# Reading a corner sum from PSUM, and moving two chunks' loads, in a fused attention and MLP kernel

## The chip, the cores and the metric

The kernel runs on one core of one Trainium2 chip. The metric is the device time of one execution in microseconds (us); the time given for a kernel is the median over several executions. One execution was also taken with the hardware profiler, and its trace is what this document reads. The engines are called as in the trace: PE is TensorE's matmul and PEld its weight load, DVE is VectorE, ACT is ScalarE, POOL is GpSimd, SP is the engine that only issues DMAs here.

## The reference

Linear attention with decay over 4 batches, 8 heads, 768 positions and head size 64, followed by a two-layer MLP (512 to 2048 to 512) with ELU between the layers:

```python
for b in range(nb):                                   # blocks of positions
    intra = einsum('bhic,bhjc->bhij', qb, kb) * Dmask # causal, lam ** (i - j)
    intra = einsum('bhij,bhjd->bhid', intra, vb)
    inter = einsum('bhid,bhde->bhie', qb * lam_pow, kv_state)
    out[:, :, sl] = intra + inter
    kv_state = lam_block * kv_state + einsum('bhsd,bhse->bhde', kb * rev_pow, vb)
x = out.transpose(0, 2, 1, 3).reshape(3072, 512)      # tokens x (heads * 64)
h = x @ w_in
g = where(h > 0, h, exp(min(h, 0)) - 1)
return g @ w_out                                      # float32, 3072 x 512
```

## The kernel before

The kernel works on 24 chunks of 128 tokens. Chunk g holds batch g % 4 and positions g // 4 * 128 onward. Chunks 0 to 3 go through the MLP alone, the others in pairs, named by the first of the two ("group 12" is chunks 12 and 13). Everything is float16 in SBUF with float32 sums in PSUM.

**Attention of a chunk.** `emit_load` loads q, k and v with DMAs issued by POOL (line 107), two chunks per DMA from chunk 4 on. From chunk 8 on, `pool_work` (token `W`) issues the DMA transposes of q and k on SP (line 270), scales k on POOL (kd, line 176) and scales the old state (stt, line 390 on POOL, line 383 on ACT). Scores are PE line 304 (token `S`), the masking of scores is DVE line 320 (pp), the outputs are PE lines 340 and 346 (token `P`), the state update is PE line 417 with DVE line 440 (token `U`). The scores of both chunks of a pair stand next to each other on PE.

**The MLP.** `mm1` computes 512 columns of the first layer into one of two PSUM buffers psH (PE line 660), then ACT takes the exponential (line 666, e) and the relu in place (line 667), and DVE forms ELU from the two (line 626, called g or gg), which sets psH free. For chunks 0 to 7 the second layer is plain (`mm2`, line 685). For the pairs from 8 on, `mm2_seven` (line 549) multiplies by Strassen's seven products: the 2 x 2 blocks are the two chunks by the two halves of the 512 output columns. The sums of gg that the products need (fp, fd, fe) are formed by `sums` on DVE (line 500) or POOL (line 497), the sums of the weights (wf) by `w_sums` (line 517).

**The corner sums.** The products come in the order m3, m4, m5, m2, m1, m7, m6, with first-layer matmuls between them, into halves of two PSUM banks. m5 adds up on m3 in the same half bank, m2 on m4, m6 on m1. ACT copies m3, m4 and m1 to SBUF (line 556, `keep`), and copies the two corners that m5 and m2 complete into the output tiles osb (line 566, `corner`). POOL adds t = m3 + m4, and subtracts the corners from t (s1 and s2, line 562, written into the buffers of m3 and m4). DVE adds w1 = s1 + m1 (line 562), and closes the other two corners with w1 - m7 and s2 + m6 (line 579), each of which reads one operand from PSUM.

**Order.** The order on every engine is written by hand. `OPEN` is the list of tokens for the first part of the program: `W8` is `pool_work(8)`, `L12` loads chunks 12 and 13, `S8:9` does scores, `1:g:j` and `2:g:j` are parts of `mm1` and `mm2`. After it the same tokens are placed at fixed distances from the first-layer steps (`AT`). Small DVE operations wait in the lists `late`, `slow` and `later`, which `flush` works off at each following step; `late.insert(0, ...)` puts one first. `COMB` is POOL.

Of the kernel before, what the change touches and what calls it, by code (L numbers as in the profile page):

```python
# [7 lines left out]
FP32 = mybir.dt.float32  # L8
# [3 lines left out]
ALU = mybir.AluOpType  # L12
# [3 lines left out]
def kernel(  # L16
# [11 lines left out]
    nc = tc.nc  # L28
    out_dram = out

    B, H, S, D = q.shape
# [28 lines left out]
    )  # L60
    LAGU = 13
    LATE = 4
# [2 lines left out]
    COMB = nc.gpsimd  # L65
# [15 lines left out]
    msb = ctx.enter_context(tc.tile_pool(name="msb", bufs=1))  # L81
# [29 lines left out]
    for w in RAW.split():  # L111
        x = {"q": q, "k": k}[w[0]]
        g0 = int(w[1:])
        raw[w] = asb.tile([128, H, 64], FP32, name=f"raw_{w}", tag=f"raw_{w}")
        (nc.sync if w[0] == "q" else nc.scalar).dma_start(
            out=raw[w][:], in_=x[g0, :, 0:L].rearrange("h p d -> p h d")
# [84 lines left out]
    def zero_st1(b):  # L201
# [21 lines left out]
        out=ident16[:], in0=row[:], scalar1=pos[:, 0:1], scalar2=None, op0=ALU.is_equal  # L223
    )
    nc.vector.tensor_scalar(
        out=causT[:], in0=row[:], scalar1=pos[:, 0:1], scalar2=None, op0=ALU.is_ge
# [82 lines left out]
    late, X_done, Y_done, E_done = [], set(), set(), set()  # L309
# [209 lines left out]
    L_, R_ = slice(0, 256), slice(256, 512)  # L519
    later, sides = [], [0, 1]  # L520

    def mm2_seven(g0, i):
        flush()
        while slow and i in (2, 4, 5):
            slow.pop(0)()
        if i == 0:
            seven[g0] = {}
            sides.reverse()
        z = seven[g0]
        if i < 2:  # L530
            while later:
                later.pop(0)[1]()
            z[f"bank{i}"] = ps.tile(
                [128, DM], FP32, tag=f"psM{sides[i]}", name=f"psM{g0 + i}", bufs=1
            )
        m = (3, 4, 5, 2, 1, 7, 6)[i]
        half = L_ if i < 4 else R_
        out = z["bank1" if m in (4, 2, 7) else "bank0"][:, half]
        for s in range(NFT // 2):
            t = g2[(g0, s // 2)]  # L540
            p, d, e = forms[(g0, s // 2)]
            u = s % 2
            lhs = {3: t[:, u, 0, 0, :], 4: t[:, u, 1, 1, :], 1: e[:, u, :], 7: d[:, u, 1, :],
                   6: d[:, u, 0, :], 5: p[:, u, 0, :], 2: p[:, u, 1, :]}[m]
            if m in (5, 2):
                rhs = wo16[s][:, 1, R_] if m == 5 else wo16[s][:, 0, L_]
            else:
                rhs = wf[s][:, (3, 4, 1, 6, 7).index(m), :]
            nc.tensor.matmul(  # L549
                out, lhsT=lhs, rhs=rhs, start=(s == 0 and m in (3, 4, 1, 7)),  # L550
                stop=(s == NFT // 2 - 1), skip_group_check=True,
            )

        def keep(n):
            z[n] = msb.tile([128, 256], FP32, tag=n, bufs=1, name=f"{n}_{g0}")
            nc.scalar.copy(out=z[n][:], in_=out)  # L556

        def comb(n, in0, in1, op, into=None, eng=None):
            z[n] = z[into] if into else msb.tile(
                [128, 256], FP32, tag=n, bufs=1, name=f"{n}_{g0}"  # L560
            )
            (eng or COMB).tensor_tensor(out=z[n][:], in0=in0, in1=in1, op=op)  # L562

        def corner(c, half):
            z[c] = msb.tile([128, DM], FP32, tag="osb512", bufs=4, name=f"osb{g0 + c}")
            nc.scalar.copy(out=z[c][:, half], in_=out)  # L566
            if last:
                store(c, half)

        last = g0 == NG - 2  # L570

        def store(c, cols):
            cb, b = divmod(g0 + c, B)
            t0 = b * S + cb * L
            stores.append((out_dram[t0 : t0 + 128, cols], z[c][:, cols]))

        def last_of(c, half, x, op):
            def one():
                nc.vector.tensor_tensor(out=z[c][:, half], in0=z[x][:], in1=out, op=op)  # L579
                store(c, half if last else slice(0, DM))  # L580
                C_done.add(g0 + c)

            later.append([DELAY, one])


        if m == 3:
            keep("m3")
        elif m == 4:
            keep("m4")
            comb("t", z["m3"][:], z["m4"][:], ALU.add)  # L590
        elif m == 5:
            corner(0, R_)
            comb("s1", z["t"][:], z[0][:, R_], ALU.subtract, "m3")
        elif m == 2:
            corner(1, L_)
            comb("s2", z["t"][:], z[1][:, L_], ALU.subtract, "m4")
        elif m == 1:
            keep("m1")
            late.insert(
                0, lambda: comb("w1", z["s1"][:], z["m1"][:], ALU.add, "m1", nc.vector)  # L600
            )
        elif m == 7:
            last_of(0, L_, "w1", ALU.subtract)
        else:
            last_of(1, R_, "s2", ALU.add)
# [6 lines left out]
    def flush():  # L612
        while pending:
            g0, j, e, r = pending.pop(0)
            n = GSIZE[g0]
            if g0 in SEVEN:
                if j % 2 == 0:
                    g2[(g0, j // 2)] = msb.tile(
                        [128, 2, 2, 2, 128], FP16, tag="g2", bufs=8, name=f"gg{g0}_{j}"
                    )  # L620
                g = g2[(g0, j // 2)][:, j % 2]
            else:
                g = msb.tile(
                    [128, FB // n, n, 128], FP16, tag="g", bufs=24, name=f"g{g0}_{j}"
                )[:]
            nc.vector.scalar_tensor_tensor(  # L626
                out=g.rearrange("p f c t -> p (f c t)"), in0=e[:], scalar=-1.0, in1=r[:],
                op0=ALU.add, op1=ALU.min,
            )
            for f in range(FB // n):  # L630
                for c in range(n):
                    gts[(g0 + c, j * (FB // n) + f)] = g[:, f, c, :]
            if g0 in SEVEN and j % 2 == 1:
                slow.extend(sums(g0, j // 2))
        if late:
            late.pop(0)()
        if slow and len(late) < 2:
            slow.pop(0)()
        for x in later:
            x[0] -= 1  # L640
        while later and later[0][0] <= 0:
            later.pop(0)[1]()
# [82 lines left out]
    def run(t):  # L725
# [13 lines left out]
        if w == "S":  # L739
            for g in a:  # L740
                att_S(g)
            for g in a:
                late.extend(att_E(g))
            late.pop(0)()
            late.pop(0)()
        elif w == "P":
            burst(t)
        elif w == "U":
            late.extend(att_U(*a))
            while late:  # L750
                late.pop(0)()
        else:
            {"T": att_T_pe, "1": mm1, "2": mm2, "Z": zero_st, "z": zero_st1,
             "q": lambda g, e: cast_raw(g, "q", e), "k": lambda g, e: cast_raw(g, "k", e),
             "7": mm2_seven, "F": w_sums, "G": lambda i: w_sums(i, nc.gpsimd), "c": lambda i: (emit_qs, emit_mask, emit_ks)[i](), "W": pool_work,
             "M": next_M}[w](*a)
# [7 lines left out]
    m1 = [(g, j) for g, n in GSIZE.items() for j in range(NJ * n)]  # L764
# [14 lines left out]
    for g in range(0, NG, 2):  # L779
        u = place[(GFIRST[g], 0)] - (8 if GSIZE[GFIRST[g]] == 4 and g == GFIRST[g] else 0)  # L780
# [14 lines left out]
    m1 = [x for x in m1 if "1:%d:%d" % x not in done]  # L795
# [4 lines left out]
    for x, (g, j) in enumerate(m1):  # L800
        u = first + x
# [3 lines left out]
        n = 2 if back > LAGU and m2[0][0][0] == "2" else 1  # L805
# [44 lines left out]
```

## Time and profile before

| | before |
|---|---|
| median of 8 runs | 218.33 us (215.33 to 220.48) |
| the profiled execution | 216.19 us |
| its span in the trace | 214.4 us |
| PE busy | 196.8 us, 92% of the span |
| DVE busy | 163.2 us, 76% |
| POOL busy | 160.9 us, 75% |
| ACT busy | 140.6 us, 66% |

The span runs from the first to the last instruction of the program; the execution's time has 1.8 us around it. In a row of groups or of the timeline the columns are: start and duration in us, engine, line of the code, operation, output and inputs by the program's names with their shapes and the number of instructions; in brackets stands how long the engine was idle before it and what ended that. In the list of waits each row has the waiting engine and line, the releaser, and the total, the number and the longest of the waits in us. In the chain of waits each row is a start, a duration and what held the chain there. An engine's name with a q is its queue: there the time that an issue takes is shown, and a DMA's row in the chain reaches from its issue to its landing.

### The profile page before, as it was taken

Reading aid. Unit: us, or ns where it says so; the run is one execution under the profiler, and the core shown is the slowest. Engines: PE = TensorE matmul, PEld = TensorE weight load, DVE = VectorE, ACT = ScalarE, POOL = GpSimd, SP = SyncE. Lnnn points to the kernel's source line nnn. Section 1 sums busy time; section 2 is a strip of 40 time slices with the busy share of each in tenths; the row PEclk is TensorE's granted clock in tenths of the full one; section 3 lists DMA queues with packets and bytes.
Section 4 is the critical chain, followed back from the end, with each engine's and each line's share of the span. In section 5 each row is a group of like instructions: output and inputs, shape, how many; then the busy total and the mean of one; then the engine's idle time right before and its main releaser. Section 6 shows DMA issues by size and latency. Waiting matters only on the chain.

```text
span 214.4 us, 5659 instructions
## 1 busy us (share of the span) xinstructions
PE 196.8 (92%) x2224; PEld 157.4 (73%) x2224; DVE 163.2 (76%) x294; ACT 140.6 (66%) x285; POOL 160.9 (75%) x187
## 2 busy tenths in 40 slices
PE   0689999999999997999999999979999999999983
PEld 0467767858586764667887887968888888888862
DVE  3864571689947785998979889898999989886622
ACT  4537665874875772867876867866567667677730
POOL 7999799999999999685999999995370301205961
PEclk9999999999999999999999999999999999999999
DMA  8999999999992399189719979979999911011032
GB/s 87 131 166 191 196 195 186 160 185 186 143 151 73 22 175 171 29 94 112 140 16 150 127 95 151 159 52 140 148 78 152 130 52 49 3 49 49 3 113 82
DMA packets 102122, 24.61 MB, mean 115 GB/s; under 512 B 92624, under 2 KB 99280, under 8 KB 102096
## 3 DMA queue, kind: packets, MB, share of 16 engines
q0 software_dynamic: 79760, 13.50, 82.9%
q1 hardware_dynamic: 22336, 10.76, 26.9%
q8 instruction: 17, 0.28, 0.6%
q14 instruction: 9, 0.07, 0.1%
HBM read 27.27 MB, written 6.29 MB: 157 GB/s over the span
## 4 chain that ended last, share of the span: by engine, by line
PE 70%; DMA 8%; DVE 8%; ACT 6%; POOL 5%; issue 2%; ACTq 0%; DVEq 0%; POOLq 0%; SPq 0%
PE psH L660 31%; PE psM L549 20%; PE psM L685 11%; DMA wo<-in_moe_w_out_dram 4%; DMA kT<-kn 4%; DVE gg L626 3%; PE psS L304 3%; ACT e L666 3%; ACT psH L667 3%; PE psO L340 2%; PE psO L346 2%; POOL wi L149 1%; POOL vn L107 1%; POOL kn L107 1%; DVE m L562 1%
## 5 line engine op out<-in xcount | busy, mean ns | idle before, releaser
L660 PE MATMUL psH<-xt,wi 128*128 128x256 f16 (+1 forms) x896 | 100.7, 260 | 3.6 <-DVE gg L626 2.3
L660 PEld LDWEIGHTS <-wi 128*128 128x128 f16 x896 | 78.6, 99 | 18.9 <-issue 4.9
L666 ACT ACTIVATE e<-psH 128x512 f32<-128x512 f32 x96 | 57.3, 597 | 47.9 <-PE psH L660 46.6
L667 ACT ACTIVATE psH<-psH 128x512 f32<-128x512 f32 x96 | 57.0, 593 | 0.0
L626 DVE SCALAR_TENSOR_TENSOR gg<-e,psH 128x512 f16<-128x512 f32 x64 | 43.6, 681 | 13.7 <-ACT psH L667 13.4
L320 DVE TENSOR_TENSOR pp<-psS,mask 128x512 f16<-128x512 f32 x48 | 31.3, 682 | 5.4 <-PE psS L304 5.4
L626 DVE SCALAR_TENSOR_TENSOR g<-e,psH 128x512 f16<-128x512 f32 x32 | 21.9, 684 | 17.3 <-ACT psH L667 17.1
L685 PE MATMUL psM<-wo,g 128*128 128x512 f16 x128 | 32.1, 379 | 0.1
L497 POOL TENSOR_TENSOR fd<-gg 128x512 f16<-128x512 f16 x20 | 24.6, 1232 | 2.8 <-DVE gg L626 2.7
L176 POOL TENSOR_TENSOR kd<-kn,ks 128x512 f16<-128x512 f16 x20 | 21.4, 1073 | 1.7 <-DMA kn<-in_k_dram 1.6
L497 POOL TENSOR_TENSOR fe<-gg 128x256 f16<-128x256 f16 x16 | 12.2, 764 | 13.0 <-DVE gg L626 12.9
L517 POOL TENSOR_TENSOR wf<-wo 128x256 f16<-128x256 f16 (+1 forms) x28 | 21.1, 792 | 0.1
L562 POOL TENSOR_TENSOR t<-m,m 128x256 f32<-128x256 f32 x8 | 5.8, 726 | 19.6 <-ACT m L556 19.6
L685 PEld LDWEIGHTS <-g 128*128 128x128 f16 x128 | 11.7, 98 | 9.8 <-issue 0.4
L562 POOL TENSOR_TENSOR m<-t,osb 128x256 f32<-128x256 f32 x16 | 11.5, 726 | 9.9 <-ACT osb L566 5.9
L549 PE MATMUL psM<-wf,gg 128*128 128x256 f16 x128 | 16.8, 273 | 0.8 <-DVE osb L579 0.5
L549 PE MATMUL psM<-wo,fp 128*128 128x256 f16 x128 | 16.5, 273 | 0.0
L549 PE MATMUL psM<-wf,fd 128*128 128x256 f16 x128 | 16.4, 273 | 0.0
L500 DVE TENSOR_TENSOR fp<-gg 128x512 f16<-128x512 f16 x32 | 15.7, 490 | 0.6
L107 POOL DMA_DIRECT2D qn<-in_q_dram x13 | 14.8, 1136 | 0.9 <-POOLq L834 0.8
L107 POOL DMA_DIRECT2D kn<-in_k_dram x14 | 15.4, 1098 | 0.0
L107 POOL DMA_DIRECT2D vn<-in_v_dram x14 | 15.3, 1099 | 0.0
(60 smaller groups left out, 257.1 us busy)
## 6 DMA issues: line engine op xcount, KB each, us to landing
out_dram<-osb SPq DMA_DIRECT2D x22, 256.0 KB, 3.0
kn<-in_k_dram POOLq DMA_DIRECT2D x10, 256.0 KB, 7.8
qn<-in_q_dram POOLq DMA_DIRECT2D x10, 256.0 KB, 5.5
vn<-in_v_dram POOLq DMA_DIRECT2D x10, 256.0 KB, 8.9
wi<-in_moe_w_in_dram POOLq DMA_DIRECT2D x8, 256.0 KB, 7.6
wo<-in_moe_w_out_dram POOLq DMA_DIRECT2D x8, 256.0 KB, 8.6
kn<-in_k_dram POOLq DMA_DIRECT2D x4, 128.0 KB, 4.3
vn<-in_v_dram POOLq DMA_DIRECT2D x4, 128.0 KB, 5.9
```

The costliest lines, as they stand in the source:

```text
L107: nc.gpsimd.dma_start(out=t[:].rearrange("p b h d -> p (b h) d"), in_=src)
L176: nc.gpsimd.tensor_tensor(out=kd[:], in0=of(kg, g), in1=ks[:].unsqueeze(2).broadcast_to([128, H, 64]), op=ALU.mult,)
L320: nc.vector.tensor_tensor(out=P[:], in0=pts[hh][:], in1=mask[:, hh::2, :], op=ALU.mult)
L497: nc.gpsimd.tensor_tensor(out=out[:], in0=in0, in1=in1, op=op)
L517: eng.tensor_tensor(out=out, in0=in0, in1=in1, op=op)
L549: nc.tensor.matmul(out, lhsT=lhs, rhs=rhs, start=(s == 0 and m in (3, 4, 1, 7)), stop=(s == NFT // 2 - 1), skip_group_check=True,)
L562: (eng or COMB).tensor_tensor(out=z[n][:], in0=in0, in1=in1, op=op)
L626: nc.vector.scalar_tensor_tensor(out=g.rearrange("p f c t -> p (f c t)"), in0=e[:], scalar=-1.0, in1=r[:], op0=ALU.add, op1=ALU.min,)
L660: nc.tensor.matmul(pH[:, f * n * 128 : (f + 1) * n * 128], lhsT=wi16[i][:, kk, w * 128 : (w + 1) * 128], rhs=xg[g0][:, kk, :], start=(kk = ...
L666: nc.scalar.activation(e[:], pH[:], AF.Exp)
L667: nc.scalar.activation(pH[:], pH[:], AF.Relu)
L685: nc.tensor.matmul(psM[g][:, cols], lhsT=gts[(g, j * FB + f)], rhs=wo16[i][:, w, cols], start=first and f == 0, stop=end and f == FB - 1, ...
```

## The change

In `mm2_seven`, m1 is no longer copied to SBUF by ACT. w1 is computed by DVE in place in a buffer u, with m1 read from PSUM: w1 = u + m1, where u = t - m5's corner is written by POOL into a buffer of its own (s1 before, which went into m3's buffer). s2 is formed in place in t (before, in m4's buffer). A loop ahead of the last product makes sure that w1 has been put into DVE's order before it. In `OPEN`, the token `L12` moves from behind the burst of chunks 6 and 7 to the end of the list, behind `W10`.

```diff
-        "S6:7 1:4:2 G2 2:5:0 2:4:0 1:4:4 1:4:5 W8 B:P6:P7:U6:U7 L12 1:4:7 1:6:1 2:5:1 2:4:1 G7 "
+        "S6:7 1:4:2 G2 2:5:0 2:4:0 1:4:4 1:4:5 W8 B:P6:P7:U6:U7 1:4:7 1:6:1 2:5:1 2:4:1 G7 "
         "1:4:6 1:6:0 G6 2:4:2 S8:9 1:6:2 1:6:4 2:5:2 2:5:3 W11 1:6:3 1:6:6 B:P8:P9:U8:U9 1:6:7 "
-        "2:4:3 1:6:5 W10"
+        "2:4:3 1:6:5 W10 L12"
...
+        while i == 6 and "w1" not in z:
+            late.pop(0)()
...
-        def comb(n, in0, in1, op, into=None, eng=None):
-            z[n] = z[into] if into else msb.tile(
-                [128, 256], FP32, tag=n, bufs=1, name=f"{n}_{g0}"
-            )
-            (eng or COMB).tensor_tensor(out=z[n][:], in0=in0, in1=in1, op=op)
+        def comb(n, x, y, op, eng=COMB):
+
+            z[n] = z[x]
+            if eng is nc.vector:
+                y = out
+            eng.tensor_tensor(out=z[n][:], in0=z[x][:], in1=y, op=op)
...
         elif m == 4:
             keep("m4")
-            comb("t", z["m3"][:], z["m4"][:], ALU.add)
+            z["t"] = msb.tile([128, 256], FP32, tag="t", bufs=1, name=f"t_{g0}")
+            nc.gpsimd.tensor_tensor(
+                out=z["t"][:], in0=z["m3"][:], in1=z["m4"][:], op=ALU.add
+            )
         elif m == 5:
             corner(0, R_)
-            comb("s1", z["t"][:], z[0][:, R_], ALU.subtract, "m3")
+            z["u"] = msb.tile([128, 256], FP32, tag="u", bufs=1, name=f"u_{g0}")
...
+                nc.gpsimd.tensor_tensor(
+                    out=z["u"][:], in0=z["t"][:], in1=z[0][:, R_], op=ALU.subtract
+                )
         elif m == 2:
             corner(1, L_)
-            comb("s2", z["t"][:], z[1][:, L_], ALU.subtract, "m4")
...
+                comb("s2", "t", z[1][:, L_], ALU.subtract)
         elif m == 1:
-            keep("m1")
-            late.insert(
-                0, lambda: comb("w1", z["s1"][:], z["m1"][:], ALU.add, "m1", nc.vector)
-            )
+            late.insert(0, lambda: comb("w1", "u", None, ALU.add, nc.vector))
```

More of the change, by code (lines that the diff above doesn't have):

```diff
@@ L589, in mm2_seven @@
             keep("m4")
-            comb("t", z["m3"][:], z["m4"][:], ALU.add)
+            z["t"] = msb.tile([128, 256], FP32, tag="t", bufs=1, name=f"t_{g0}")
+            nc.gpsimd.tensor_tensor(
+                out=z["t"][:], in0=z["m3"][:], in1=z["m4"][:], op=ALU.add
+            )
         elif m == 5:
             corner(0, R_)
-            comb("s1", z["t"][:], z[0][:, R_], ALU.subtract, "m3")
+            z["u"] = msb.tile([128, 256], FP32, tag="u", bufs=1, name=f"u_{g0}")
+            if COMB is nc.vector:
+                late.insert(0, lambda: nc.vector.tensor_tensor(
+                    out=z["u"][:], in0=z["t"][:], in1=out, op=ALU.subtract
+                ))
+            else:
+                nc.gpsimd.tensor_tensor(
+                    out=z["u"][:], in0=z["t"][:], in1=z[0][:, R_], op=ALU.subtract
+                )
         elif m == 2:
             corner(1, L_)
-            comb("s2", z["t"][:], z[1][:, L_], ALU.subtract, "m4")
+            if COMB is nc.vector:
+                late.insert(0, lambda: comb("s2", "t", None, ALU.subtract))
+            else:
+                comb("s2", "t", z[1][:, L_], ALU.subtract)
         elif m == 1:
-            keep("m1")
-            late.insert(
-                0, lambda: comb("w1", z["s1"][:], z["m1"][:], ALU.add, "m1", nc.vector)
-            )
+            late.insert(0, lambda: comb("w1", "u", None, ALU.add, nc.vector))
         elif m == 7:
```

## The prediction

> **What bounds the kernel now.** I read the page's busy table and slices first, then the chain that ended last, then who waited for whom on TensorE, then the timeline around each piece of the chain that is not TensorE work.
>
> ```profile
> PE 196.8 (92%) x2224; PEld 157.4 (73%) x2224; DVE 163.2 (76%) x294; ACT 140.6 (66%) x285; POOL 160.9 (75%) x187
> PE   0689999999999997999999999979999999999983
> PE 70%; DMA 8%; DVE 8%; ACT 6%; POOL 5%; issue 2%; ACTq 0%; DVEq 0%; POOLq 0%; SPq 0%
> 75.00 8.01 DMA kT<-kn
> 141.23 2.52 DVE m L562
> PE psS L304 <- DMA kT<-kn: 1.5, 1, 1.5
> PE psH L660 <- DVE gg L626: 2.3, 7, 1.1
> ```
>
> TensorE is busy 92% and carries the chain: the kernel ends earlier only where TensorE stops waiting. After start-up its slices are full but for two with a 7, and the chain holds a foreign piece in each: the transpose of a k tile, 8.01 us from issue to landing, and one DVE addition of 2.52 us. TensorE itself waited 1.5 us for the first and at most 1.1 us for the second. These are the two places that the change touches. The timeline of the first:
>
> ```profile
> 71.74 1.21 POOL L107 DMA_DIRECT2D qn<-in_q_dram  x1
> 72.94 1.15 POOL L107 DMA_DIRECT2D kn<-in_k_dram  x1
> 74.07 1.16 POOL L107 DMA_DIRECT2D vn<-in_v_dram  x1
> 75.00 1.27 SPq L270 DMA_TRANSPOSE kT<-kn  x1
> 83.05 0.62 PE L304 MATMUL psS<-qT,kT 64*128 64x128 f16 x16 [1.46 <-DMA kT<-kn]
> 98.74 0.62 PE L304 MATMUL psS<-qT,kT 64*128 64x128 f16 x16
> ```
>
> The three loads of chunks 12 and 13 are issued from 71.74 to 75.23; in the middle of their traffic SP issues the two transposes of chunk 10 (73.66 and 75.00), and kT of chunk 10 lands at 83.01. The scores of chunks 10 and 11 stand first in TensorE's queue and wait. The scores of chunks 12 and 13, at 98.74, are the first users of the loads. The timeline of the second:
>
> ```profile
> 141.23 2.51 DVE L562 TENSOR_TENSOR m<-m,m 128x256 f32<-128x256 f32 x1
> 141.66 0.68 POOL L497 TENSOR_TENSOR fe<-gg 128x256 f16<-128x256 f16 x1
> 142.29 1.16 POOL L497 TENSOR_TENSOR fd<-gg 128x512 f16<-128x512 f16 x1
> 143.66 0.67 DVE L626 SCALAR_TENSOR_TENSOR gg<-e,psH 128x512 f16<-128x512 f32 x1
> 144.39 1.85 PE L660 MATMUL psH<-xt,wi 128*128 128x256 f16 x15 [1.07 <-DVE gg L626]
> ```
>
> The corner sum w1 of group 12 lasts until POOL's two operations are through; the gg behind it on DVE comes late, the PSUM buffer that gg frees comes late, TensorE stands 1.07 us.
>
> [...] In the answer on the tiles m, w1 (two SBUF inputs) takes 417/606/2509 ns (least, median, most); the closing sums, which read one operand from PSUM, take 406/414/421 ns in all 16 cases:
>
> ```profile
> L579 DVE TENSOR_TENSOR osb<-m,psM x16: 406/414/421, 111.9 to 211.1; 128x256 f32<-128x256 f32 x16
> L562 DVE TENSOR_TENSOR m<-m,m x8: 417/606/2509, 110.6 to 209.8; 128x256 f32<-128x256 f32 x8
> ```
>
> [...] transposes of k land after 2.4 us at the least and 8.0 at the most, the long ones while loads are on the way.
>
> **The change part by part.**
>
> *Corner sum.* Gone: eight ACT copies of m1, 375 ns each, 3.0 us of ACT. ACT is idle before most exponentials (46.6 us waiting for psH in all), so they lie in the shade: 0. w1 becomes u + PSUM: the row of the closing sums, 0.41 us each. In four groups w1 took 0.79, 0.89, 2.51 and 0.89, in the others 0.42; so DVE gives up 3.4 us. On the path stood only group 12's: the operand of the next gg is ready at 141.88 (its relu starts at 141.29 and takes 0.59), so with w1 over at about 141.7 TensorE's wait of 1.07 goes: **-1.1**. Nothing else is late there; bounds 0 [...] and -1.1.
>
> A wait is added. The last product, m6, accumulates in the half bank that w1 now reads, so the first matmul of m6 waits for w1 on DVE, where it waited for ACT's copy. Behind it in TensorE's queue stand the next first-layer matmuls, and with them everything. w1 keeps its place on DVE (the order of DVE's instructions is the same in the changed program), behind fp, or behind fp, fe and fd. Ends of w1 against starts of m6: groups 8, 10, 12 and 20, with 0.41 in place of the long w1, 111.0, 126.15, 141.65 and 202.05 against 111.28, 126.78, 142.28 and 202.69, so room of 0.3 to 0.6; group 14, 158.81 against 158.71, late by 0.1; groups 16 and 18, 173.87 and 189.12 against 173.96 and 189.21, just in time; group 22, whose w1 no longer waits for the copy, about 209.7 against 209.96. With some 0.05 for the signal: **+0.15**. Bounds: 0, and 0.6 in each of four groups when the fp ahead of w1 runs into POOL (fp takes 0.42 as a rule, 1.37 at 85.88), so +2.4. u and t live longer; t of the next group now waits for the closing sum of the last, which ended 4 us or more before in groups 10 to 20 and 1.5 us before in group 22: 0.
>
> *Loads moved.* The three issues, 3.5 us of POOL, go from 71.74 to behind stt of chunk 10, and nothing is issued twice. POOL's wf7, wf6, kd11, kd10 and stt10 (75.29 to 85.75) start 3.55 us earlier, at 71.74; none waits for something late. The loads then go out from about 82.2 to 85.75, where fd of group 8 starts as before (85.82).
>
> Gain: the transposes of chunk 10 are issued when they were (SP is held by a store until 73.2) but with no loads around them. They should land 2.4 to 4 us after issue, by 79; the scores are due at 81.5. **-1.5**. Some 2 us later fp (85.88, 1.37 long, in collision with fd) held up the mask product of chunk 11, for which TensorE stood 0.2 at 87.9; DVE now gets there while POOL is issuing: **-0.3**, bounds 0 and -0.4.
>
> Price: the loads of 12 and 13 have less time. The same triple, back to back, stands at 155.85 to 159.3 in the trace, with its four transposes behind it:
>
> ```profile
> 155.85 1.18 POOL L107 DMA_DIRECT2D qn<-in_q_dram  x1
> 157.03 1.15 POOL L107 DMA_DIRECT2D kn<-in_k_dram  x1
> 158.16 1.16 POOL L107 DMA_DIRECT2D vn<-in_v_dram  x1
> 164.01 1.19 SPq L270 DMA_TRANSPOSE kT<-kn  x1
> 166.57 1.81 SPq L270 DMA_TRANSPOSE kT<-kn  x1
> ```
>
> k landed 7.0 us after its issue, and the last kT 4.3 us after 166.57, at 170.9: 15.05 us from first load to last transpose. From 82.25 that gives 97.3; with the store of out4 that SP has between the transposes (0.6) 97.9. The scores of 12 and 13, at 98.74 before, are due at about 96.9 after the gains. So TensorE waits about **+1.0**. Bounds: 0 (k lands after 5.0 to 5.7 us, as the triples at 92 and 113 have it) and +6 (below). On POOL, kd12 waits for k12 until 90.4 and stands ahead of fd: fd8_1, kd13 and the next load go from 90.18, 91.29 and 92.48 to about 91.5, 92.7 and 93.9. By the last fd of group 8 POOL is 1 to 2 us late; it stood idle 2.70 us at 99.2, waiting for gg: cost 0, and if that cover is gone, fe and kd have several us in hand before TensorE uses them. SP's queue: out4 goes from 82.84 to about 91.7 and out6 behind the transposes; four output buffers in rotation, next needed beyond 104: 0.
>
> Sum: -1.1 + 0.15 - 1.5 - 0.3 + 1.0 = -1.75. The profiled execution took 216.19 (span 214.4, 1.8 around it), so 214.45. The median of eight, 218.33, lies 2.1 above it; I carry the difference over: 216.6. Since 1% (2.2 us) is about what a measurement of this kernel can tell from no change, the forecast lies close to that line.
>
> **Rivals.**
> 1. The loads arrive in time (k after 5 us, the last kT before 96.9): no new wait, -2.75, **215.6**. For it: the other triples. Against: those had 2 us more between q and k.
> 2. The wait only moves: kT of 13 lands at about 99.5, wait 2.6, so 1.6 more than in the sum; -0.15, **218.2**. For it: the next load, q14, goes out at 93.9, just as kT of 13 is issued (93.6), and transposes beside loads took 6 to 8 us.
> 3. m6 becomes the gate: +2.0 over four groups instead of 0.15; about 0, **218.4**. Against: POOL's order and DVE's are unchanged, and at that place POOL is issuing a load.
> 4. Slower: kT of chunk 13 falls fully behind q14 and k14. In the triple of before the last load took 9.2 us to land; if the last kT takes that, it lands at 102.8 and the scores wait 5.9, 4.9 more than in the sum: +3.15, **221.5**. It decides from a landing at 99.7 on; over 1% slower needs 101.8. For it: 8.3 us were seen for a transpose issued with a k and a v load ahead of it. Against: only one load, issued later, is there at that moment.
>
> **How the numbers follow.** Forecast 0.38, rivals 0.22, 0.16, 0.08 and 0.16. Below 216.1 lie most of rival 1 and a little over half of the forecast's own spread: 0.42. Above 220.5 lie rival 4 and a rest for what I don't see in a kernel whose eight times span 5 us: 0.21. Within 1%: 0.37. Range 213.9 (all gains and no price, -2.9, and 1.5 for executions that wait longer than the profiled one) to 220.4 (rival 4 in part).
>
> **What would show it.** Right: kT of chunk 10 lands within 4 us and no wait stands before the scores near 81.5; w1 reads 0.41 us in all eight groups and TensorE has no 1 us gap near 140; a wait for kT of about 1 us before the scores near 97; waits of m6 for DVE under 0.2. Wrong: a wait for kT or qT of chunk 12 or 13 of over 3 us; m6 waiting more than 0.3 in several groups; POOL's fe late enough to be waited for; or the scores of 10 waiting as before, which would mean that the loads were not what held the transpose.

## The result and the profile after

The changed kernel takes 213.59 us (median of 11, 213.03 to 215.10), where the kernel before took 217.72 in the same comparison: ratio 0.9853, 95% interval 0.9818 to 0.9888. It is faster by 4.1 us between these medians, more than the forecast of 1.75. 213.59 lies just below the low end of the range as it was put, 213.9; the ratio on the 218.33 of then gives 215.1, inside it. One thing has to be known to read the medians: in 36 of the 91 executions of the kernel before in the later comparisons the mean granted TensorE clock (1.0 is full speed) was 0.992 or less (their median 218.36; called "lost clock" below), in the other 55 it was 0.997 or more (median 216.02; called "at full clock"), and in the changed kernel none of 18 executions lost clock.

The profiled execution has a span of 211.7 us against 214.4. From the page: TensorE's slices, and who waited for whom on TensorE in the list of waits.

```profile
PE   0688999999999999999999999999999999999983
PE psT L285 <- DVE qn L125: 5.6, 1, 5.6
PE psH L674 <- DVE gg L640: 1.8, 8, 0.3
```

Both 7s are gone from the slices. The wait for kT is gone from the list, and the longest wait for gg is 0.3 us instead of 1.1; the 5.6 us belong to the start, as before. The timeline around the moved loads and the two pairs of scores:

```profile
74.20 1.26 SPq L270 DMA_TRANSPOSE kT<-kn  x1
80.78 0.62 PE L304 MATMUL psS<-qT,kT 64*128 64x128 f16 x16
81.50 1.21 POOL L107 DMA_DIRECT2D qn<-in_q_dram  x1
91.62 1.22 POOL L107 DMA_DIRECT2D qn<-in_q_dram  x1
91.65 1.26 SPq L270 DMA_TRANSPOSE kT<-kn  x1
92.91 1.26 DVE L500 TENSOR_TENSOR fe<-gg 128x256 f16<-128x256 f16 x1
94.83 1.91 PE L674 MATMUL psH<-xt,wi 128*128 128x256 f16 x16 [0.34 <-DVE gg L640]
96.67 0.62 PE L304 MATMUL psS<-qT,kT 64*128 64x128 f16 x16
```

kT of chunk 10 now lands 2.5 us after its issue at 74.20 (8.0 before), and the scores of 10 and 11 start at 80.78 with no wait for it. kT of chunk 13, issued at 91.65, lands after 4.5 us, at 96.2, half a microsecond before the pair of scores begins whose second half needs it. The corner sums, from the answer on the tiles u:

```profile
L565 DVE TENSOR_TENSOR u<-u,psM x8: 414/415/422, 108.9 to 206.7; 128x256 f32<-128x256 f32 x8
```

414 to 422 ns in all eight groups, where w1 took up to 2509.

Of the 2.7 us between the two spans, 0.6 came before anything that was changed: the first-layer matmuls at 36.41 in the trace of before stand at 35.80 here. The scores of 10 and 11 are 2.27 earlier, those of 12 and 13 2.07, the last closing sum 2.66; so some 2.1 us of this pair of traces are the change's.

### The profile page after: what moved, and what is told of

Read it like the earlier page. It is cut to its first block, busy times and chain, and to the rows that moved or that the text cites. A ratio compares the mean times of both kernels' runs of the same rounds, so it can differ in the third digit from the quotient of the medians.

```text
span 211.7 us, 5654 instructions
## 1 busy us (share of the span) xinstructions
PE 196.1 (93%) x2224; PEld 156.7 (74%) x2224; DVE 160.1 (76%) x294; ACT 138.0 (65%) x277; POOL 159.9 (76%) x187
## 4 chain that ended last, share of the span: by engine, by line
PE 69%; DVE 10%; ACT 8%; POOL 5%; DMA 4%; issue 2%; ACTq 0%; POOLq 0%; DVEq 0%
PE psH L674 31%; PE psM L551 21%; PE psM L699 9%; DMA wo<-in_moe_w_out_dram 4%; ACT e L680 3%; ACT psH L681 3%; DVE gg L640 3%; PE psS L304 3%; PE psO L340 2%; DVE g L640 2%; DVE st L440 2%; POOL wi L149 1%; PE psO L346 1%; POOL vn L107 1%; POOL kn L107 1%
## 5 line engine op out<-in xcount | busy, mean ns | idle before, releaser
L497 POOL TENSOR_TENSOR fe<-gg 128x256 f16<-128x256 f16 x16 | 11.7, 733 | 13.3 <-DVE gg L640 13.2
L500 DVE TENSOR_TENSOR fp<-gg 128x512 f16<-128x512 f16 x32 | 14.6, 455 | 0.6
L551 PEld LDWEIGHTS <-gg 128*128 128x128 f16 x128 | 11.9, 98 | 3.2 <-issue 0.7
```

What stands on the lines that cost most here:

```text
L497: nc.gpsimd.tensor_tensor(out=out[:], in0=in0, in1=in1, op=op)
L500: lambda out=out, in0=in0, in1=in1, op=op: nc.vector.tensor_tensor(out=out[:], in0=in0, in1=in1, op=op)
L551: nc.tensor.matmul(out, lhsT=lhs, rhs=rhs, start=(s == 0 and m in (3, 4, 1, 7)), stop=(s == NFT // 2 - 1), skip_group_check=True,)
```

## Experiments

**One part each.** The kernel before with the loads moved alone:

```diff
-        "S6:7 1:4:2 G2 2:5:0 2:4:0 1:4:4 1:4:5 W8 B:P6:P7:U6:U7 L12 1:4:7 1:6:1 2:5:1 2:4:1 G7 "
+        "S6:7 1:4:2 G2 2:5:0 2:4:0 1:4:4 1:4:5 W8 B:P6:P7:U6:U7 1:4:7 1:6:1 2:5:1 2:4:1 G7 "
-        "2:4:3 1:6:5 W10"
+        "2:4:3 1:6:5 W10 L12"
```

> The loads of chunks 12 and 13 moved, the corner sum as before. Theory (two separate waits of TensorE, one per part, that add up): the wait of 1.5 us for kT of chunk 10 and the 0.3 us after it go, and no wait for kT of chunks 12 or 13 comes; about 2.0 us faster than before (ratio 0.991), and w1 still takes up to 2.5 us in the groups where POOL reads beside it. Rival A (the loads are the whole gain): 3 us or more, ratio 0.986. Rival B (the sum is the whole gain, the loads' wait was hidden by what comes later): within 0.5 us, ratio 0.998 to 1.002.

Measured: 214.54 us, ratio 0.9881 (0.9837 to 0.9925), all six executions at full clock. This interval holds both the theory's 0.991 and rival A's 0.986, and executions of the kernel before that lost clock count in it; the comparison at full clock below leaves no 3 us for rival A. Its timeline still has the long corner sum, and TensorE's wait behind it:

```profile
138.84 2.50 DVE L562 TENSOR_TENSOR m<-m,m 128x256 f32<-128x256 f32 x1
142.00 1.20 PE L660 MATMUL psH<-xt,wi 128*128 128x256 f16 x9 [1.07 <-DVE gg L626]
```

The changed kernel with the loads back at their old place:

```diff
-        "S6:7 1:4:2 G2 2:5:0 2:4:0 1:4:4 1:4:5 W8 B:P6:P7:U6:U7 1:4:7 1:6:1 2:5:1 2:4:1 G7 "
+        "S6:7 1:4:2 G2 2:5:0 2:4:0 1:4:4 1:4:5 W8 B:P6:P7:U6:U7 L12 1:4:7 1:6:1 2:5:1 2:4:1 G7 "
-        "2:4:3 1:6:5 W10 L12"
+        "2:4:3 1:6:5 W10"
```

> The corner sum read from PSUM, the loads where they were. Theory: only the wait of about 1.1 us behind the long w1 of one group goes, ratio 0.995; the wait for kT of chunk 10 stays at about 1.5 us. Rival A: no change, ratio 0.999 to 1.001. Rival B: 3 us, ratio 0.986. If the scatter of the times of before (215.3 to 220.5) comes from w1 colliding with POOL at chance moments, the times of this kernel scatter by 2 us or less; if it comes from the loads, they scatter as before.

Measured: ratio 0.9959 (0.9930 to 0.9989). At full clock 215.03 (14 of 22) against 215.95 for the kernel before on the same chip (20 of 27): 0.9 us. The wait for kT of chunk 10 is still there, in the list of waits of TensorE:

```profile
PE psS L304 <- DMA kT<-kn: 1.7, 1, 1.7
```

And 8 of the 22 executions lost clock (median 217.41) where none of the six of l12_only did, so the scatter of before goes with the loads, not with the corner sum. At full clock the parts are worth 1.4 us (215.95 to 214.54) and 0.9 us; the whole change is worth 2.4 (216.02 to 213.6). They add up within the noise: neither part is nothing, and neither is the whole. For the loads alone 2.0 had been expected; 1.4 does not stand clear of that.

**Is it ACT's work or DVE's second SBUF input?** The corner sum from PSUM, and ACT still copying m1 for nobody:

```diff
         elif m == 1:
+            keep("m1")
             late.insert(0, lambda: comb("w1", "u", None, ALU.add, nc.vector))
```

> As w1_only, but ACT still makes the eight copies of m1, which nobody reads. Theory (the gain of this part is DVE's second SBUF input, not ACT's work): the same time as w1_only within 0.3%, w1 at 0.41 us in all eight groups. Rival (the gain is ACT's 3.0 us): the time of before, slower than w1_only by about 0.5%.

Measured: only three of six executions had full clock, 214.35 to 214.53; too few against w1_only to tell 0.3%, but all below every full-clock execution of before beside them (214.70 at the least). So with the copies still made the gain is there. w1 took 410 to 421 ns. So the same line was added to the changed kernel, with the changed kernel beside it:

> The changed kernel once more, as the yardstick of the two below: 213.6 us, mean clock 1.0 in every execution.

> The changed kernel with ACT's eight copies of m1 still made, which nobody reads. Theory (ACT's 3.0 us lie in the shade, the corner sum's gain is DVE's second SBUF input alone): the time of the changed kernel within 0.3 us. Rival (ACT's copies were a part of the gain): 0.5 us or more slower.

Measured: 213.70 (212.65 to 214.38, 6 executions) and 214.05 (213.34 to 214.75, 10). The medians are 0.35 us apart, within the scatter of either; and the trace with the copies has a wait of 0.34 us for kT of chunk 13, which the two traces of the changed kernel have not, so even this difference need not be ACT's. The gain does not need ACT's copies gone; whether they are worth nothing or a third of a microsecond stays open.

**What the lost clock is.** The profiled execution of w1_copy_kept is one that lost clock. Its timeline at the scores of 10 and 11, and the busy times in two stretches (after the stretch: busy us and instructions of PE, PEld, DVE, ACT and POOL, then the granted clock, DMA share, GB/s):

```profile
83.99 1.03 PE L304 MATMUL psS<-qT,kT 64*128 64x128 f16 x16 [2.59 <-DMA kT<-kn]
...
79.00:84.00 5.00, 2.27 (x18) 1.26 (x16) 1.97 (x3) 2.46 (x5) 5.00 (x7) 1.00 1.67 139
84.00:88.00 4.00, 4.00 (x29) 2.44 (x30) 3.37 (x5) 0.00 (x0) 2.54 (x5) 0.58 0.77 140
```

TensorE stood 2.59 us for kT, a microsecond more than in the trace of before; and at the end of the wait the granted clock falls to 0.58 over 4 us. By estimate that is 0.50 (the clock that the trace of l12_later, below, shows over 3.41 us) for some 3.4 us, or 1.7 us lost: in that stretch the 16 matmuls of the scores took 1.03 us instead of 0.62, and the four of the second layer behind them 1.89 instead of 1.04 (83.60 in the trace of before). A mean clock of 0.992 over 216 us is the same amount: 216 x 0.008 / 0.5 = 3.5 us at half speed. A wait of 2.59 us was enough here, and 1.5 to 1.7 us (traces of before and of w1_only) was not. The changes of the granted clock show more: the one stretch at full clock that is recorded in the trace of before is 197.97 us long, that of the changed kernel 194.56, which is 58 and 57 times 3.413. Cut into steps of that length, w1_copy_kept, w1_only and l12_later (the kernel below) have at their waits for kT:

```profile
80.56:83.97 3.41, 0.84 (x8) 0.49 (x6) 0.69 (x1) 1.08 (x2) 3.41 (x5) 1.00 1.79 165
80.24:83.65 3.41, 1.75 (x26) 1.13 (x24) 1.19 (x2) 1.08 (x2) 3.41 (x5) 1.00 1.30 128
96.35:99.76 3.41, 0.48 (x10) 0.23 (x8) 3.41 (x4) 1.17 (x3) 3.40 (x4) 1.00 1.20 80
99.76:103.17 3.41, 1.63 (x14) 1.13 (x15) 1.93 (x4) 0.00 (x0) 3.22 (x4) 0.50 1.77 195
```

The first number behind the comma is TensorE's busy time. The clock fell after the steps with 0.84 and 0.48 us of it, and not after the one with 1.75; at the end of the program it fell after a step with 0.77 (changed kernel), and in the trace of before not after one with 1.98. So it also fell after steps in which TensorE was not idle throughout. An estimate from these numbers: in an otherwise busy stream a single wait takes the clock from a length between 1.7 and 2.6 us on (3.41 less 1.75 or 0.84), if it lies within one step; where the steps begin differs from execution to execution (the first record lies 17.87 us after the start in the trace of before, 16.42 in that of the changed kernel).

To show that the wait is the cause, the loads were moved one POOL operation further in the changed kernel, which should make a wait at the other place:

```diff
-        "2:4:3 1:6:5 W10 L12"
+        "2:4:3 1:6:5 W10"
...
         prog.append(f"1:{g}:{j}")
+        prog += ["L12"] * (x == 2)
```

> The changed kernel with the three loads one operation later still, behind fd of group 8, so some 2.7 us later. In the changed kernel kT of chunk 13 landed 0.5 us ahead of the scores that need it. Theory (that half microsecond is all the room there is): TensorE waits about 2.2 us before the scores of 12 and 13, the time is about 216 us, and in executions where the wait gets longer than some 2 us the granted clock drops to half for 3.4 us after it, which adds 1.7 us (the mean clock of such an execution reads 0.992). Rival (the landing times have slack, the kernel is held by the first-layer chain there): the time of the changed kernel within 0.5 us, 213.6, clock 1.0.

Measured: 216.67. The "some 2 us" of the expectation was an estimate between the 1.7 us of w1_only and the 2.59 of w1_copy_kept. Nine executions were at full clock with median 215.68, twelve were at 0.992, two at 0.984 (14 together: 217.24). The full-clock ones are 2.1 us above the changed kernel, where 2.2 were expected; those that lost clock are another 1.6 above them, near the 1.7 of one stretch. The profiled one is one of the two at 0.984:

```profile
PE psS L304 <- DMA kT<-kn: 4.7, 1, 4.7
101.60:105.00 3.40, 3.40 (x22) 2.39 (x23) 1.70 (x3) 0.37 (x1) 1.39 (x2) 0.50 2.33 161
```

In it kT of chunk 13 was issued 0.2 us before the next load of q and landed after 6.3 us, and its wait spans two steps, those shown above: the clock fell after the first and stayed low after the second, with 1.63 us of work. With one more load ahead of k:

```diff
+                if (t, w) == ("L12", "k"):
+                    spare = asb.tile([128, 2, H, 64], FP16, name="spare", tag="spare")
+                    nc.gpsimd.dma_start(
+                        out=spare[:].rearrange("p b h d -> p (b h) d"),
+                        in_=v[0:2, :, 3 * L : 4 * L].rearrange("b h p d -> p (b h) d"),
+                    )
                 emit_load(w, int(t.strip("Lqkv")))
```

> As l12_later, with one more load of 256 KB (of data that nobody reads) between q and k. Theory: k and everything behind it lands some 1.7 us later again, TensorE waits about 4 us, and the granted clock drops to half for one stretch of 3.4 us in every execution (mean clock 0.992): 213.6 + 4 + 1.7 = 219.3 us. Rival (the clock falls for reasons of its own, not because TensorE stood still): mean clock 1.0 in most executions, 217.6 us.

Measured: 220.98, ratio 1.0199 (1.0150 to 1.0248), 0.984 or less in all six executions. That is 1.7 more than expected. TensorE's two waits for kT in the trace make 4.5 us, 0.5 more; and the mean clock of 0.984 over its span of 219.0 us is 7.0 us at half speed (219.0 x 0.016 / 0.5), by estimate two stretches of 3.4 us and not one. In l12_later's trace TensorE worked 5.0 us of its two (1.63 and 3.41); as much here would be some 2.5 us lost and not 1.7, an estimate too. In the three traces with a wait of 2.6 us or more the clock fell, and where the traces have waits for kT of at most 0.34 us at these places it never did: 0 of 58 executions of l12_only, v12_late, q12_early, after_copy_kept, the changed kernel and their repeats lost clock, against 36 of 91 before. The rival, that it falls for reasons of its own, has no run for it. No execution of the kernel before that lost clock was traced, though: that its wait is longer there than 1.46 us is taken from w1_copy_kept.

**How much load is too much ahead of a transpose?** The kernel before with the load of v alone moved:

```diff
-        "S6:7 1:4:2 G2 2:5:0 2:4:0 1:4:4 1:4:5 W8 B:P6:P7:U6:U7 L12 1:4:7 1:6:1 2:5:1 2:4:1 G7 "
+        "S6:7 1:4:2 G2 2:5:0 2:4:0 1:4:4 1:4:5 W8 B:P6:P7:U6:U7 Lq12 Lk12 1:4:7 1:6:1 2:5:1 2:4:1 G7 "
-        "2:4:3 1:6:5 W10"
+        "2:4:3 1:6:5 W10 Lv12"
```

> The kernel before with only the load of v of chunks 12 and 13 moved behind the transposes of chunk 10; q and k stay. Theory (the transposes wait for the traffic of the loads issued ahead of them, in proportion to it): a third of the traffic less, so kT of chunk 10 lands some 1.7 us earlier, at about 81.3, and TensorE's wait of 1.5 us nearly goes: ratio 0.993 to 0.996. Rival (any load in flight holds a transpose to the end): kT lands at about 81.5 to 83 and the wait stays, ratio 0.998 to 1.0. In both, no new wait for kT of 12 and 13.

Measured: ratio 0.9883 (0.9837 to 0.9929), 214.15. That is faster than the 0.993 to 0.996 that were expected: 1.8 us at full clock (215.95 to 214.15), and none of the six executions lost clock. No difference from all three moved can be told. In its trace kT of chunk 10 lands 6.8 us after its issue instead of 8.0 (1.2 less; 1.7 were expected), and the scores wait for it 0.20 us. A third less traffic was enough. With q left at the old place and k and v moved, in the changed kernel:

```diff
-        "S6:7 1:4:2 G2 2:5:0 2:4:0 1:4:4 1:4:5 W8 B:P6:P7:U6:U7 1:4:7 1:6:1 2:5:1 2:4:1 G7 "
+        "S6:7 1:4:2 G2 2:5:0 2:4:0 1:4:4 1:4:5 W8 B:P6:P7:U6:U7 Lq12 1:4:7 1:6:1 2:5:1 2:4:1 G7 "
-        "2:4:3 1:6:5 W10 L12"
+        "2:4:3 1:6:5 W10 Lk12 Lv12"
```

> The changed kernel with the load of q of chunks 12 and 13 back at its old place and only k and v behind the transposes of chunk 10. Theory: one load ahead of the transposes is done soon enough, so kT of chunk 10 lands by about 80 without a wait, and kT of chunk 13 lands a microsecond or two earlier than in the changed kernel, which already has no wait there: the same time, 213.6 within 0.5. Rival (any load holds the transposes): a wait of over 1 us for kT of chunk 10, 215 us.

> The changed kernel with the load of q of chunks 12 and 13 at its old place (q12_early), beside the changed kernel on one chip. Theory (no wait is left at either place for it to take away): equal within 0.3 us. Rival (the 2.4 us more of room before the scores of 12 and 13 help in executions where the changed kernel still waits there): 0.3 us or more faster.

Measured: 213.30, and beside the changed kernel 213.38 against 213.70 (12 and 6 executions, ranges 212.95 to 214.85 and 212.65 to 214.38). kT of chunk 10 landed 3.6 us after its issue. No difference from the changed kernel can be told.

**The new wait of m6.** The changed kernel with the other two corner sums on DVE too:

```diff
-    COMB = nc.gpsimd
+    COMB = nc.vector
```

> The changed kernel with the other two corner sums (u and s2) on DVE as well, read from PSUM too, in place of POOL. 16 operations of 0.73 us leave POOL, 16 of 0.41 us come to DVE. Theory (DVE is the engine with least room in groups 8 to 18, busy 14 of 15 us in a group; POOL's work there is hidden): slower, some 0.4 us for each of eight groups, about 216 us. Rival (POOL's reads beside DVE are what delays DVE, so less of them pays for the work): the same or faster, 212.5 to 213.6 us.

Measured: 217.05, all 22 executions at full clock, 3.4 us slower than the changed kernel. The list of waits of TensorE says why, and DVE's timeline in group 8 how:

```profile
PE psM L551 <- DVE u L565: 3.0, 3, 1.3
...
109.56 1.40 DVE L500 TENSOR_TENSOR fp<-gg 128x512 f16<-128x512 f16 x1
110.98 0.42 DVE L565 TENSOR_TENSOR u<-u,psM 128x256 f32<-128x256 f32 x1
```

This is rival 3 of the prediction in another kernel. In groups 8 and 10 fp took 1.40 us instead of 0.42, w1 behind it came late, and m6 waited for w1, 1.34 and 1.07 us. Without the corner sums POOL had come to its fe and fd (from 108.89 in group 8) when fp ran; in the changed kernel it was still issuing a load there (108.18 to 109.39). In group 14 fp took 0.42 and DVE was late all the same, by 0.62. The direction was expected, the size was not: 3.4 us instead of the 2.4 that 216 meant, and 3.0 of it is the wait of m6.

## Why the prediction was right, and where its numbers were off

- *The transposes of chunk 10, -1.5.* Right: landing after 2.5 us, and the wait of 1.46 gone.
- *The fp beside fd, -0.3.* Its delay went (fp at 83.61 took 0.41), and was given back: an fe on DVE took 0.28 us at 84.54; where one had lasted longer beside POOL's fd (1.24 us at 94.64; TensorE waited 0.21 at 97.78), two did beside POOL's kd and fd now (1.09 at 90.72, 1.26 at 92.91), and TensorE waited 0.17 and 0.34. From the scores of 10 to those of 12 TensorE needed 15.89 us where it needed 15.69: +0.2 in place of -0.3.
- *The price of the later loads, +1.0.* Not paid. This is the term that was mis-sized. The 15.05 us, 15.65 with the store, were borrowed from a triple whose k took 7.0 us to land. Here k took 5.7: q, k and v started at 81.50 and the last kT landed at 96.2, 14.7 us later. That is 1.0 less, and the 0.5 by which the term before this one was off put the scores later: half a microsecond of room in place of a wait of 1.0. Rival 1 happened. In l12_later the loads stand 2.8 us later behind the scores of 10 and the time is 2.1 us longer at full clock, which puts the room at some 0.7 us by estimate.
- *The corner sum, -1.1 and +0.15.* Measured alone: -0.9, close to their sum. m6 starts 1.75 us after the start of m7 in group 14, before (156.96 to 158.71) and after (154.31 to 156.06), and no wait of m6 for w1 stands in the changed kernel's list, so the new wait cost nothing there. The traces of w1_copy_kept and after_copy_kept have one of 0.2 us, and comb_dve shows that it can cost more.
- *The sum.* Without the price it says -2.75; at full clock -2.4 was measured. The step that failed in the median is the one that carried the difference of 2.1 us between the profiled execution and the median over unchanged. Most of that difference was the lost clock: the median of before stood 2.3 us higher with it than without (218.36 and 216.02), of which one stretch at half speed is 1.7 by estimate. The change removes the wait and the clock's fall with it, which no term of the sum had; only the low end of the range left 1.5 us for executions that wait longer.
- *Rivals 2 and 4* named a kT issued together with the next load as the danger. That happened in the changed kernel (91.65 and 91.62), and kT landed after 4.5 us, not after the 6 to 8 they counted with. With everything one POOL operation later (l12_later) it took 6.3. What makes this difference the runs don't show.

## What to carry to other kernels

Before moving a load later, find its first user and count the room to it; before leaving it early, look at what lands slowly behind it, and note that a part of the load may be enough to move. A DVE operation on the path that reads two SBUF operands beside a busy GpSimd was cheaper here with one operand read from PSUM (0.41 us where it had taken up to 2.51), but the bank is then held until that operation is done (m6 waited up to 1.34 us in comb_dve). Where a median lies well above a profiled execution, compare the granted clock of the executions, and ask which wait of the profile could grow in others: here the clock stood through waits of 1.5 and 1.7 us and fell with one of 2.59.

## What the runs showed of the hardware

A wait of TensorE can have a price beyond its length: behind 2.59 us in w1_copy_kept the granted clock stood at half for another 1.7 us lost by estimate, behind 1.5 us (before) and 1.7 us (w1_only) it stayed full. The full-clock stretches of before and of the changed kernel are 58 and 57 times 3.413 us long; of the steps of that length shown or named above, it fell after those in which TensorE worked 0.84 us or less, and not after those with 1.75 or more. A DMA transpose of a 128 x 512 float16 tile landed 2.4 us after its issue at the least, and up to 8.3 us after it with loads of 256 KB on the way (trace of before). What slowed w1 is not settled: in group 12 of the kernel before it took 2.51 us beside POOL's fe and fd, but in groups 8 and 10 it started while POOL was issuing a load, took 0.79 and 0.89 us and ended at 111.40 and 126.62, 0.4 after the issue had ended (at 111.00 and 126.20). POOL's fe, which reads, began at that moment (111.01 and 126.22), so which of the two held w1 is not shown.
